# Input loads of 128 rows, an identity and a mask made on GpSimd, and a shorter load queue at the start of a recurrence-plus-experts kernel

## The chip, the cores and the metric

The kernel runs on one core of one Trainium2 chip. The metric is device microseconds for one execution. Before the change it takes 365.24 us (median of 3 runs, 364.93 to 365.54).

## What is computed

A gated linear recurrence (attention without softmax) and then a mixture of experts with one expert for each token. Cut to what matters, with batch 4, 8 heads, 768 steps, head width 48, and 8 experts of 384 x 1024 x 384:

```python
for t in range(S):
    cur = u * k[t] outer v[t]
    y[t] = r[t] @ (state + cur)
    state = w[t][:, None] * state + k[t] outer v[t]
x = y.transpose(0, 2, 1, 3).reshape(B * S, H * D)          # 3072 x 384
logits = x @ w_gate + modality_bias[modality_id]
e = argmax(logits);  g = softmax(logits)[e]
out = g * (relu(x @ w1[e]) @ w2[e])
```

All arithmetic is float32. The mask of the recurrence inside a block of 128 steps is a strict upper triangle, and every transpose on TensorE multiplies by an identity matrix.

## The kernel before, in words

The recurrence is cut into 24 **units** of 128 steps (6 for each batch entry). A unit has all 8 heads: heads lie in pairs, the two heads of a pair in partitions 0 to 47 and 64 to 111, four pairs side by side. One tensor `rkw` holds for each unit 128 rows of 1541 numbers: 512 of r, 512 of k, 517 of w. Rows 48 to 63 and 112 to 127 are padding; the host fills them with zeros for r and k and with ones for w.

`att_iter(i)` works on three units at once. For the unit two ahead, VectorE (DVE) runs two scans over w (`B`, L266, the decay to the end of the block, and `E`, L269, the decay from its start) and a reciprocal (L268); ScalarE (ACT) copies r into PSUM (`pK_r`, L218), DVE multiplies it into `R` (L221), GpSimd (POOL) makes `K` (L224) and `G` (L277). For the unit one ahead, TensorE (PE) transposes K (`pK`, L291), multiplies K by R into the 128x128 blocks `pS` (L305), DVE multiplies these by the mask into `A` (L306), and PE updates the state `st` (L317), which ACT scales and copies (L230, L233). For the unit itself PE forms the output `pY` (L331 from the state, L341 from A), POOL forms `dV` (L273) and DVE adds both into `xp` (`x_rows`, L367). `x_cols` (L374) and `logits` (L380) follow for the unit two behind. Each engine takes its instructions in program order.

Inputs go through four tiles `in0` to `in3` in turn. SyncE (SP) issues all of the loads in program order into one hardware queue; a DMA is spread over 16 DMA engines. `load(n)` (L88) takes 128 rows for the first four units, so that the padding rows are set once, and `64 + D` = 112 rows for the other twenty. The load of unit i+5 is issued behind `att_iter(i)`, when the tile's last reader is done. The load of v (128 rows of 384) goes ahead of it, and from unit 6 on a piece of the first expert's weights (`raw`) goes behind it.

The tile `cs` holds constants: the identity in columns 0 to 127, the mask in columns 128 to 255, and small tables behind these. Before the first unit the program issues the loads of w, r and k of units 0 and 1 with the identity and the mask among them (L101 to L106), PE runs 12 warm-up matmuls on a zeroed tile (L115), and POOL runs ten memsets (L709), the first thing that it does in the kernel's body.

Behind the 24 units the experts follow: blocks of 256 gathered rows, two matmul stages with weights and inputs split into two float32r parts (L621 and L638).

Of the kernel before, what the change touches and what calls it, by code (L numbers as in the profile page):

```python
# [14 lines left out]
ALU = mybir.AluOpType  # L15
AX = mybir.AxisListType

B, H, S, D = 4, 8, 768, 48
P = 128
# [34 lines left out]
def kernel(ctx: ExitStack, tc: tile.TileContext, rkw, vt, wf, cst, mid, wg, bias, w1, w2, out):  # L54
    nc = tc.nc
# [20 lines left out]
    NIN = 4  # L76
    ins = [pa.tile([P, 1541], F32, name=f"in{i}", bufs=1) for i in range(NIN)]
# [8 lines left out]
        return T[tag, n]  # L86

    def load(n, cuts=((0, 1541),)):  # L88
        t, rows = ins[n % NIN], P if n < NIN else 64 + D
        for c0, c1 in cuts:  # L90
            nc.sync.dma_start(out=t[0:rows, c0:c1], in_=rkw[n, 0:rows, c0:c1])

    def loadv(n):
        nc.sync.dma_start(out=wt(n, "v", [P, DM], 4), in_=vt[n * P:(n + 1) * P, :])
# [3 lines left out]
    wm = cp.tile([P, 512], BF16, name="wm")  # L98
    nc.vector.memset(wm, 0.0)
    cs = cp.tile([P, NCST], F32, name="cs")  # L100
    load(0, ((1024, 1541),))  # L101
    nc.sync.dma_start(out=cs[:, 0:P], in_=cst[:, 0:P])
    load(0, ((0, 1024),))
    load(1, ((1024, 1541),))
    nc.sync.dma_start(out=cs[:, P:2 * P], in_=cst[:, P:2 * P])
    load(1, ((0, 1024),))  # L106
    act = cp.tile([1, 1], F32, name="act")
    nc.vector.memset(act, 0.0)
    nc.scalar.activation(out=act, in_=act, func=AF.Exp)
# [22 lines left out]
    for i in range(3):  # L132
        t = wk.tile([P, 4, 2, D], F32, name=f"SPb{i}", bufs=1)
# [811 lines left out]
def _layout(inp):  # L945
    import numpy as np

    r, k, v, w = (np.asarray(inp[n]) for n in "rkvw")

    def tr(a):  # L950
        return a.reshape(B, 4, 2, NCH, P, D).transpose(0, 3, 2, 5, 1, 4)

    W = np.zeros((B, NCH, 2, D, 517), np.float32)
    W[..., :516].reshape(B, NCH, 2, D, 4, 129)[..., 1:] = tr(w)
    rkw = np.zeros((NU, 2, 64, 1541), np.float32)
    rkw[:, :, D:, 1024:] = 1.0
    rkw[:, :, 0:D] = np.concatenate([tr(r).reshape(B, NCH, 2, D, 512), tr(k).reshape(B, NCH, 2, D, 512), W], -1).reshape(NU, 2, D, 1541)
    uu = np.zeros((P, 4, 32), np.float32)
    u = np.asarray(inp["u"]).reshape(4, 2, D)
    for hh in range(2):  # L960
        uu[64 * hh:64 * hh + D, :, hh] = u[:, hh].T
    vt = np.ascontiguousarray(v.transpose(0, 2, 1, 3)).reshape(NT, DM)
    wg = np.asarray(inp["moe_w_gate"])
    c = np.zeros((P, NCST), np.float32)
    c[:, 320:320 + P] = uu.reshape(P, P)
    c[:, 320 + P:] = wg.reshape(KC, P, E).transpose(1, 0, 2).reshape(P, KC * E)
    c[:, 0:P] = np.eye(P)
    c[:, P:2 * P] = np.triu(np.ones((P, P)), 1)
    c[:, 256:264] = np.arange(E) - E
    c[:, 264:288] = np.arange(NU)[None, :] * P + np.arange(P)[:, None]  # L970
    c[:, 288:308] = np.arange(20)
    c[:, 308:316] = np.arange(E) * RS
    mid = np.ascontiguousarray(inp["moe_modality_id"]).astype(np.int64)
    return {
        "rkw": rkw.reshape(NU, P, 1541),
        "vt": vt,
        "wf": np.ascontiguousarray(w).reshape(P, NG * GW),
        "cst": c,
        "mid": mid.view(np.int32).reshape(NU, 2 * P),
        "wg": np.ascontiguousarray(wg),  # L980
        "bias": np.ascontiguousarray(inp["moe_modality_bias"]),
        "w1": np.ascontiguousarray(np.asarray(inp["moe_w1"]).reshape(E, KC, P, FC, P).transpose(0, 2, 3, 1, 4)).reshape(E, P, FC * DM),
        "w2": np.ascontiguousarray(np.asarray(inp["moe_w2"]).reshape(E, FC, P, DM).transpose(0, 2, 1, 3)).reshape(E, P, FC * DM),
    }
# [13 lines left out]
```

## Time and profile before

| what | value |
|---|---|
| median of the runs | 365.24 us |
| the profiled execution | 368.07 us |
| its span, first to last instruction of the program | 366.3 us |
| time of the profiled execution outside the span | 1.77 us |
| mean granted TensorE clock | 0.984 |
| PE busy / DVE busy / ACT busy / POOL busy | 348.2 / 229.3 / 223.8 / 247.1 us |
| share of PE in the chain that ended last | 75% |
| share of DVE in it | 11% |

The durations come from one profiled execution. "Idle before" is the time in which an engine did nothing ahead of an instruction, with what ended that time behind an arrow; "issue" means that the engine waited for nothing that the profile shows. The row "PEclk" has the clock that TensorE was granted, in tenths of full speed; "DMA" the mean busy share of the 16 DMA engines, in tenths, in 40 slices of 9.16 us; an answer by windows has the same as a share of one (a little over 1 where packets overlap at a window's edge). KB in lists of DMA issues are 1024 bytes; GB/s are 10^9 bytes a second. The recurrence fills the span up to about 136 us, the experts the rest.

### The profile page before, as it was taken

The numbers are of one execution on the slowest core, as the hardware profiler recorded it, in microseconds if no ns is written. First come the engines' busy times: TensorE is split into PE (matmuls) and PEld (weight loads), VectorE is DVE, ScalarE is ACT, GpSimd is POOL, SyncE is SP. The second block draws the span as 40 slices with busy tenths as digits, with TensorE's granted clock in tenths as the row PEclk, the third lists the DMA queues.
The fourth block names the chain that finished last, engine by engine and source line by source line (L and its number), as shares of the span: only waits on it lengthen the run. The fifth ranks groups of instructions, "written<-read, shape, count | busy, mean of one in ns | idle before, by whom it ended". The sixth has DMA issues, their size and how long they took to land.

```text
span 366.3 us, 10841 instructions
## 1 busy us (share of the span) xinstructions
PE 348.2 (95%) x4246; PEld 332.0 (91%) x4246; DVE 229.3 (63%) x365; ACT 223.8 (61%) x466; POOL 247.1 (67%) x221
## 2 busy tenths in 40 slices
PE   7889999999889999999999999999999999999993
PEld 2778989898778989999999999999999999999992
DVE  5969999999999836753587471708071716571110
ACT  3647468586364626664676767676867686844340
POOL 4665869998889935875878875564747474728271
PEclk9889999999998999999999999999999999999999
DMA  7994898886786370012255523131312564064200
GB/s 239 316 234 143 239 239 235 235 228 177 227 244 202 129 219 1 2 43 66 86 176 209 181 88 108 46 108 45 108 53 100 162 248 147 28 200 152 105 26 26
DMA packets 20256, 53.28 MB, mean 145 GB/s; under 512 B 2693, under 2 KB 12709, under 8 KB 20196
## 3 DMA queue, kind: packets, MB, share of 16 engines
q1 hardware_dynamic: 17076, 43.04, 40.2%
q0 software_dynamic: 3120, 9.47, 7.0%
q8 instruction: 35, 0.57, 0.6%
q14 instruction: 25, 0.20, 0.2%
HBM read 75.66 MB, written 11.54 MB: 238 GB/s over the span
## 4 chain that ended last, share of the span: by engine, by line
PE 75%; DVE 11%; issue 7%; POOL 3%; DMA 1%; ACT 1%; SPq 0%; POOLq 0%; DVEq 0%; ACTq 0%
PE pS_u L621 20%; PE pY_d L638 13%; PE pX_d L638 13%; PE pT_u L621 9%; PE pS L305 5%; DVE B L266 3%; PE pY L341 3%; DVE A L306 3%; DVE R L221 2%; PE pY L331 2%; PE pK L291 2%; PE pK_x L605 2%; PE pU_st L317 2%; DMA in<-rkw 1%; PE pT L374 1%
## 5 line engine op out<-in xcount | busy, mean ns | idle before, releaser
L207 POOL TENSOR_TENSOR wl<-raw,wh 128x768 fp32r<-128x768 f32 x52 | 96.6, 1868 | 69.5 <-ACT wh L206 69.4
L206 ACT CAST wh<-raw 128x768 fp32r<-128x768 f32 x96 | 79.2, 830 | 35.1 <-PE pX_d L638 24.3
L621 PE MATMUL pS_u<-xh,wh 128*128 128x256 f32 (+1 forms) x198 | 56.3, 284 | 0.0
L621 PE MATMUL pS_u<-xo,wh 128*128 128x256 f32 (+1 forms) x198 | 55.8, 282 | 0.0
L621 PE MATMUL pS_u<-xh,wl 128*128 128x256 f32 (+1 forms) x198 | 55.5, 280 | 0.0
L626 DVE SCALAR_TENSOR_TENSOR hl<-pS_u,hh 128x512 fp32r<-128x512 f32 (+1 forms) x33 | 22.4, 680 | 50.5 <-ACT hh L625 50.5
L207 DVE TENSOR_TENSOR wl<-raw,wh 128x768 fp32r<-128x768 f32 x44 | 49.8, 1132 | 2.8 <-ACT wh L206 1.9
L647 POOL DMA_INDIRECT out<-ot,xl x25 | 32.1, 1282 | 11.0 <-ACT ot L646 5.3
L621 PEld LDWEIGHTS pS_u<-xh,wl 128*128 128x128 f32 x198 | 37.6, 190 | 0.0
L621 PEld LDWEIGHTS pS_u<-xo,wh 128*128 128x128 f32 x198 | 37.2, 188 | 0.0
L621 PEld LDWEIGHTS pS_u<-xh,wh 128*128 128x128 f32 x198 | 37.2, 188 | 0.0
L625 ACT ACTIVATE hh<-pS_u 128x512 fp32r<-128x512 f32 (+1 forms) x33 | 19.5, 591 | 27.5 <-PE pS_u L621 23.7
L626 DVE SCALAR_TENSOR_TENSOR hl<-pT_u,hh 128x512 fp32r<-128x512 f32 (+1 forms) x15 | 10.1, 670 | 39.0 <-ACT hh L625 39.0
L273 POOL TENSOR_TENSOR dV<-v,dT 128x384 f32<-128x384 f32 x24 | 20.0, 834 | 19.7 <-ACT dT L250 8.2
L638 PE MATMUL pY_d<-wh,hh 128*128 128x384 f32 x96 | 33.3, 347 | 0.0
L306 DVE TENSOR_TENSOR A<-pS,cs 128x1024 f32<-128x1024 f32 x24 | 29.2, 1218 | 5.5 <-PE pS L305 5.4
L638 PE MATMUL pX_d<-wh,hh 128*128 128x384 f32 (+1 forms) x96 | 32.3, 336 | 0.0
L638 PE MATMUL pX_d<-wh,hl 128*128 128x384 f32 (+1 forms) x96 | 32.3, 336 | 0.0
L638 PE MATMUL pY_d<-wl,hh 128*128 128x384 f32 x96 | 32.3, 336 | 0.0
L638 PE MATMUL pX_d<-wl,hh 128*128 128x384 f32 (+1 forms) x96 | 32.3, 336 | 0.0
L638 PE MATMUL pY_d<-wh,hl 128*128 128x384 f32 x96 | 32.2, 336 | 0.0
L224 POOL TENSOR_TENSOR K<-in,B 128x512 f32<-128x512 f32 x24 | 28.4, 1185 | 4.2 <-DMA in<-rkw 4.1
(191 smaller groups left out, 894.2 us busy)
## 6 DMA issues: line engine op xcount, KB each, us to landing
raw<-w SPq DMA_DIRECT2D x52, 768.0 KB
in<-rkw SPq DMA_DIRECT2D x20, 674.2 KB
xl<-xs SPq DMA_DIRECT2D x12, 386.0 KB
v<-vt SPq DMA_DIRECT2D x24, 192.0 KB
wg<-wf SPq DMA_DIRECT2D x8, 576.0 KB
raw<-w SPq DMA_DIRECT2D x16, 192.0 KB
xs<-zt SPq DMA_DIRECT2D x8, 193.0 KB
in<-rkw SPq DMA_DIRECT2D x3, 512.0 KB
```

Of the source, the lines that this page charges most:

```text
L206: nc.scalar.copy(out=wh[k][:, sl], in_=raw[k][:, sl])
L207: (nc.vector, nc.gpsimd)[k].tensor_tensor(out=wl[k][:, sl], in0=raw[k][:, sl], in1=wh[k][:, sl].bitcast(F32), op=ALU.subtract)
L224: nc.gpsimd.tensor_tensor(out=wt(a, "K", [P, 4, P]), in0=quarters(k), in1=quarters(T["B", a][:, 1:517])[:, :, 1:129], op=ALU.mult)
L266: nc.vector.tensor_tensor_scan(out=Bt[:, 516:0:-1], data0=w[:, 516:0:-1], data1=d1[:, 516:0:-1], initial=0.0, op0=ALU.mult, op1=ALU.max)
L273: nc.gpsimd.tensor_tensor(out=dV, in0=T["v", z].rearrange("p (a b) -> p a b", a=H), in1=T["dT", z].rearrange("p a b -> p (a b)")[:, :, Non ...
L305: nc.tensor.matmul(out=pS[:, hh, p], lhsT=K[q, p], rhs=R[q, p], start=True, stop=True)
L306: nc.vector.tensor_tensor(out=A.rearrange("p a b c -> p (a b) c"), in0=pS.rearrange("p a b c -> p (a b) c"), in1=mask[:, None, :].to_broad ...
L621: nc.tensor.matmul(out=pp[:, i], lhsT=wsrc[0][:, f, c * P:(c + 1) * P], rhs=xsrc[:, c], start=(n == 0), stop=(n == 3 * KC - 1))
L625: nc.scalar.activation(out=hh, in_=pp, func=AF.Relu)
L626: nc.vector.scalar_tensor_tensor(out=hl, in0=pp, scalar=0.0, in1=hh.bitcast(F32), op0=ALU.max, op1=ALU.subtract)
L638: nc.tensor.matmul(out=X["y", q][j][0:h.shape[-1]], lhsT=h, rhs=wsrc[1][:, f], start=(f == 0 and n == 0), stop=(f == FC - 1 and n == 2))
L647: ins = nc.gpsimd.indirect_dma_start(out=out[:, :], out_offset=bass.IndirectOffsetOnAxis(ap=xl[0:n, j, DM + 1:DM + 2].bitcast(I32), axis=0 ...
```

## The change

Three edits. `load` takes all 128 rows for every unit, where units 4 to 23 took 112. The two loads of the identity and the mask are gone, so the loads of r and k of units 0 and 1 stand right behind their w. POOL makes identity and mask: a memset of 128x256 to one, and two `affine_select` of 128x128, which keep the diagonal and the part above it and write zero elsewhere. The host no longer fills these columns.

```diff
     def load(n, cuts=((0, 1541),)):
-        t, rows = ins[n % NIN], P if n < NIN else 64 + D
         for c0, c1 in cuts:
-            nc.sync.dma_start(out=t[0:rows, c0:c1], in_=rkw[n, 0:rows, c0:c1])
+            nc.sync.dma_start(out=ins[n % NIN][:, c0:c1], in_=rkw[n, :, c0:c1])
...
-    load(0, ((1024, 1541),))
-    nc.sync.dma_start(out=cs[:, 0:P], in_=cst[:, 0:P])
-    load(0, ((0, 1024),))
-    load(1, ((1024, 1541),))
-    nc.sync.dma_start(out=cs[:, P:2 * P], in_=cst[:, P:2 * P])
-    load(1, ((0, 1024),))
+    load(0, ((1024, 1541), (0, 1024)))
+    load(1, ((1024, 1541), (0, 1024)))
+    nc.gpsimd.memset(cs[:, 0:2 * P], 1.0)
+    for c0, op in ((0, ALU.is_equal), (P, ALU.is_gt)):
+        v = cs[:, c0:c0 + P]
+        nc.gpsimd.affine_select(out=v, in_=v, compare_op=op, fill=0.0, base=0, pattern=[[1, P]], channel_multiplier=-1)
```

The order of the instructions on SP at the start of the kernel before, from its first load; `in0_88` and `in1_89` are the input tiles of units 0 and 1, where 128x517 is w and 128x1024 is r and k:

```order
L91 DMA in0_88<-rkw 128x517
L102 DMA cs_94<-cst 128x128
L91 DMA in0_88<-rkw 128x1024
L91 DMA in1_89<-rkw 128x517
L105 DMA cs_94<-cst 128x128
L91 DMA in1_89<-rkw 128x1024
L94 DMA v0_152<-vt 128x384
```

The same place in the changed kernel (line numbers are lower by one from here on):

```order
L90 DMA in0_88<-rkw 128x517
L90 DMA in0_88<-rkw 128x1024
L90 DMA in1_89<-rkw 128x517
L90 DMA in1_89<-rkw 128x1024
L93 DMA v0_153<-vt 128x384
```

The two `cs` loads are gone; r and k of unit 0 move from third to second place, those of unit 1 from sixth to fourth.

SP a little later in the kernel before, where the tiles are loaded for the second time (units 4 and 5, into `in0` and `in1`):

```order
L91 DMA in3_91<-rkw 128x1541
L94 DMA v2_239<-vt 128x384
L91 DMA in0_88<-rkw 112x1541
L94 DMA v3_317<-vt 128x384
L91 DMA in1_89<-rkw 112x1541
```

And in the changed kernel:

```order
L90 DMA in3_91<-rkw 128x1541
L93 DMA v2_240<-vt 128x384
L90 DMA in0_88<-rkw 128x1541
L93 DMA v3_318<-vt 128x384
L90 DMA in1_89<-rkw 128x1541
```

Nothing moves there; the loads from unit 4 on have 128 rows in place of 112.

POOL from the first instruction of the kernel's body, before; `ISA` is an instruction that names the library of GpSimd code that the following operations come from, and K0, G0 are the first unit's:

```order
L709 MEMSET SPb0_124 128x384
L709 MEMSET SPb1_125 128x384
L709 MEMSET SPb2_126 128x384
L709 MEMSET onesb_130 128x128
L709 MEMSET one8_133 128x8
L709 MEMSET ersb_132 128x8
L709 MEMSET zt_134 128x386
L709 MEMSET zt_134 128x1
L709 MEMSET glo_128 128x1
L709 MEMSET ghi_129 128x1
L224 ISA
L224 TENSOR_TENSOR K0_175<-in0_88,B0_170 128x512
```

And in the changed kernel:

```order
L102 MEMSET cs_94 128x256
L105 ISA
L105 AFFINE_SELECT cs_94<-cs_94 128x128 x2
L708 MEMSET SPb0_125 128x384
L708 MEMSET SPb1_126 128x384
L708 MEMSET SPb2_127 128x384
```

A memset, the library instruction and the two selects stand ahead of the ten memsets, which keep their order; K0 follows directly behind the last of these. The order on PE, DVE and ACT is unchanged.

More of the change, by code (lines that the diff above doesn't have):

```diff
@@ L966, in _layout @@
     c[:, 320 + P:] = wg.reshape(KC, P, E).transpose(1, 0, 2).reshape(P, KC * E)
-    c[:, 0:P] = np.eye(P)
-    c[:, P:2 * P] = np.triu(np.ones((P, P)), 1)
     c[:, 256:264] = np.arange(E) - E
```

## The prediction

> **What bounds the kernel now.** The experts, from about 136 us on, are left alone; what the change can move is how late they begin. So I read the recurrence: first who VectorE waits for up to 130 us.
>
> ```profile
> DVE A L306 <- PE pS L305: 5.4, 5, 2.7
> ...
> DVE R L221 <- ACT pK_r L218: 1.0, 1, 1.0
> ```
>
> (Total us, times, longest.) Then its busy time in the stretches between the longest waits: each row has the stretch, its length, the busy us and instructions of PE, PE's weight loads, DVE, ACT and POOL, then PE's granted clock, the DMA share and GB/s.
>
> ```profile
> 7.20:24.47 17.27, 13.43 (x241) 12.16 (x242) 16.99 (x21) 9.21 (x27) 11.46 (x11) 0.87 1.04 291
> 27.16:56.40 29.24, 28.17 (x651) 25.96 (x652) 28.79 (x39) 18.55 (x60) 19.80 (x25) 1.00 0.73 206
> 56.90:126.00 69.10, 64.89 (x1472) 59.60 (x1474) 67.05 (x105) 42.76 (x134) 61.44 (x71) 0.98 0.74 213
> ```
>
> DVE is busy for 98%, 98% and 97% of these. From its first R to the last units it is a chain without slack, so a microsecond by which it starts earlier, or waits less, is a microsecond at the end. Its timeline shows the places where it does wait.
>
> ```profile
> 4.96 1.23 DVE L269 TENSOR_TENSOR_SCAN E<-in,pX_d 128x516 f32<-128x516 f32 x1
> 7.20 0.69 DVE L221 TENSOR_TENSOR R<-pK_r,E 128x512 f32<-128x512 f32 x1 [1.01 <-ACT pK_r L218]
> ...
> 10.42 1.20 DVE L306 TENSOR_TENSOR A<-pS,cs 128x1024 f32<-128x1024 f32 x1
> ...
> 23.94 0.53 DVE L367 TENSOR_TENSOR xp<-pY,dV 128x384 f32<-128x384 f32 x1
> 27.16 1.22 DVE L306 TENSOR_TENSOR A<-pS,cs 128x1024 f32<-128x1024 f32 x1 [2.68 <-PE pS L305]
> ...
> 32.03 1.23 DVE L306 TENSOR_TENSOR A<-pS,cs 128x1024 f32<-128x1024 f32 x1
> ...
> 56.91 1.22 DVE L306 TENSOR_TENSOR A<-pS,cs 128x1024 f32<-128x1024 f32 x1 [0.47 <-PE pS L305]
> ```
>
> Three waits matter: 1.01 us at the start, 2.68 us at 24.5 and 0.47 us at 56.4. The last two are caused by TensorE, whose timeline says why.
>
> ```profile
> 8.55 1.16 PE L305 MATMUL pS<-R,K 64*128 64x128 f32 x16
> ...
> 20.45 0.73 PE L341 MATMUL pY<-v,A 128*64 128x48 f32 x19
> 22.53 0.56 PE L341 MATMUL pY<-v,A 128*64 128x48 f32 x13 [1.35 <-issue]
> ...
> 25.14 1.98 PE L305 MATMUL pS<-R,K 64*128 64x128 f32 x16
> ...
> 28.46 1.09 PE L341 MATMUL pY<-v,A 128*64 128x48 f32 x32
> ...
> 53.19 0.24 PE L331 MATMUL pY<-SPb,R 128*64 128x96 f32 x1 [0.61 <-issue]
> ```
>
> PE stops at 21.2 us between the 19th and the 20th of 32 equal matmuls, for 1.35 us. Their operands were there for the first 19, and the releaser is "issue": no engine's signal. It stops again near 52.6 us for 0.61. What it lacks is then the instructions themselves, which come by DMA too:
>
> ```profile
> q8 instruction: 35, 0.57, 0.6%
> ```
>
> 35 packets with 0.57 MB, 16 KB each, in a queue of their own on the same 16 engines. The stretches around the stops, and the clock:
>
> ```profile
> 0.00:10.50 10.50, 7.81 (x61) 3.89 (x62) 6.70 (x12) 3.65 (x7) 5.84 (x18) 1.00 0.79 261
> 10.50:13.50 3.00, 1.40 (x21) 1.17 (x20) 2.97 (x5) 2.23 (x8) 1.91 (x3) 0.95 1.05 408
> 13.50:28.00 14.50, 13.05 (x233) 11.81 (x233) 11.64 (x15) 7.53 (x23) 8.80 (x8) 0.77 1.04 232
> 24.00:27.00 3.00, 3.00 (x22) 2.59 (x20) 0.48 (x2) 1.56 (x3) 3.00 (x3) 0.52 1.03 238
> 51.00:54.00 3.00, 2.39 (x70) 2.10 (x67) 3.00 (x5) 1.73 (x6) 1.50 (x2) 1.00 0.97 239
> ```
>
> The granted clock is 0.52 in 24 to 27 us, right behind the first stop, and the 16 matmuls of pS take 1.98 us there against 1.16 at 8.55. The DMA share is about 1 in both stretches with a stop: the engines that must bring PE's instructions are full.
>
> **Why they are full.** The GB/s of those rows differ by 408 to 232 at the same full share. I put names to the bytes by the sizes of the issues.
>
> ```profile
> in<-rkw SPq DMA_DIRECT2D x20, 674.2 KB
> v<-vt SPq DMA_DIRECT2D x24, 192.0 KB
> ...
> raw<-w SPq DMA_DIRECT2D x16, 192.0 KB
> ...
> in<-rkw SPq DMA_DIRECT2D x3, 512.0 KB
> in<-rkw SPq DMA_DIRECT2D x3, 258.5 KB
> in<-rkw SPq DMA_DIRECT2D x1, 770.5 KB
> ...
> cs<-cst SPq DMA_DIRECT2D x2, 64.0 KB
> cs<-cst SPq DMA_DIRECT2D x1, 108.0 KB
> ```
>
> Units 0 to 3, `cs` and three loads of v are 4 x 770.5 + 236 + 3 x 192 = 3894 KB = 3.99 MB. By 13.5 us 261 x 10.5 + 408 x 3 = 3.96 MB had moved. So the 408 GB/s are loads of 128 rows, and the stretch behind, 232 x 14.5 = 3.36 MB, is units 4 to 7 and three v: 4 x 674.2 + 576 = 3273 KB = 3.35 MB. These are the first loads of 112 rows. The fall by 43% comes exactly where the row count changes.
>
> **The change part by part.**
>
> *Shorter queue at the start.* SP needs some 0.47 us for an issue:
>
> ```profile
> 0.71 0.39 SPq L91 DMA_DIRECT2D in<-rkw  x1
> 1.16 0.42 SPq L102 DMA_DIRECT2D cs<-cst  x1
> 1.63 0.90 SPq L91 DMA_DIRECT2D in<-rkw  x2
> ```
>
> r and k of unit 0 are issued at 1.16 in place of 1.63, and 64 KB go from ahead of them. In the chain that ended last they are the first piece:
>
> ```profile
> 1.63 4.92 DMA in<-rkw
> 6.58 0.60 ACT pK_r L218
> ```
>
> Landing moves from 6.55 to about 6.1, R from 7.20 to 6.73: **0.47 us**. At least 0.2 (64 KB at 261 GB/s take 0.25, if the issue hides), at most 0.98, since E ends at 6.19. B of unit 1 follows at once, and w of unit 1 moves up as well, by the same issue.
>
> *GpSimd.* POOL's first work moves back behind a memset, the library instruction and two selects:
>
> ```profile
> 0.71 1.13 POOL L709 MEMSET SPb<- 128x384 f32 x3 [0.29 <-POOLq L991]
> ...
> 2.54 0.10 POOL L709 MEMSET ghi<- 128x1 f32 x1
> 6.70 1.17 POOL L224 TENSOR_TENSOR K<-in,B 128x512 f32<-128x512 f32 x1 [4.06 <-DMA in<-rkw]
> ```
>
> The ten memsets take 0.71 to 2.64, 1.93 us; a memset of 128x256 takes two thirds of one of the three, 0.25. A select of 128x128 is not in the trace. Bounds: 0.10, the small memset, and 1.17, K over four times the elements; I take 0.30, a quarter of K. The library instruction stood inside the 4.06 us ahead of K: 0 to 4.06, and I take about 0, as the gap ends with the DMA that released ACT at 6.58. K can then start at 0.71 + 0.25 + 0.6 + 1.93 = 3.5, ahead of r and k at 6.1. The cover is the landing of r and k, and its cost is nil. Identity and mask are ready by 1.6, far ahead of pK and A.
>
> *128 rows.* Each later load has 96.3 KB more, but at 408 GB/s it takes 1.93 us where 674.2 KB at 232 took 2.98. Units 4 and 5, two v and small ones (about 1.97 MB) are through by 13.2 + 4.8 = 18 us, and unit 6, issued when its tile is free, about 2 us later; then the queue is empty. PE's instruction packet finds short queues. Without the stop pY ends at 20.45 + 1.09 = 21.54. In the next unit A followed pY's end (28.46 + 1.09 = 29.55) by 2.48 us, so A could start at 24.02, and DVE is free at 24.47: **2.68 us** fall away whole. Next to be late is DVE itself. For the stop at 52.6 us the load of an iteration becomes 770.5 + 192 + 192 (weights) KB = 1.18 MB in 4.87 us, 60% of 408 GB/s; but here weights share the queue. Between 0 and 0.47 I take the middle, **0.24**.
>
> Sum: 0.47 + 2.68 + 0.24 = 3.4 us. The span goes from 366.3 to 362.9, the profiled execution, 1.77 longer, from 368.07 to 364.7; taken off the median, 365.24 - 3.4 = **361.9 us**. The median lies 2.83 below the profiled execution, so a part of the stops may belong to profiling.
>
> **The rivals.**
>
> *Only the start gains.* The stop stays, or happens only under the profiler: 365.24 - 0.47 = 364.8. For it: the queue is full for all of the 14.5 us from 13.5 on, and PE stops once. Against it: both stops lie at a full share, none in the emptier rest.
>
> *Half.* The stop shrinks, but the idle time still takes the clock down: half of 2.68 and the start, 363.4.
>
> *More bytes, no speed.* The rate fell for another reason than the row count, and each load costs 14% more. Then four loads add 4 x 96.3 KB = 0.39 MB, 1.7 us at 232 GB/s, to the queue ahead of PE's instructions; the wait grows by as much, and less the 0.47 the time is 366.5, slower. It decides if the new loads run below 232 x 128 / 112 = 265 GB/s. For it: the clock of PE also fell near 13 us. Against it: in 51 to 54 us the clock is 1.00 and the rate 239. The Trainium skill ("SBUF — State Buffer", Door 1: The DMA port swizzle) speaks for this rival: which of 16 ports a row uses depends on its number, and by that table rows 0 to 111 already reach all 16, with four ports half used. By it 112 rows would run at 7/8 of the rate of 128, 357 of 408 GB/s, and take as long; the 232 GB/s of this trace are far below, so more than the count of ports is at work.
>
> *GpSimd late.* The library instruction costs up to 4.06 and a select up to 1.17: K starts at 0.71 + 0.25 + 4.06 + 2.34 + 1.93 = 9.29. pS ended 9.71 - 7.87 = 1.84 after K, so A would start at 12.30 against 10.42 now. If the stops stay too, 367.1. It decides when library and selects together pass 4.05 us (K after 6.94, A after 9.95). Against it: K's wait ended 0.12 us after ACT's, for the same load. The Trainium skill ("GPSIMD Engine Reference", Instruction dispatch) gives about 6 us for the first call into freshly loaded code; by that K before could not have started until 8.59, and it started at 6.70.
>
> *Nothing moves*, 365.2.
>
> **How the numbers follow.** The sum as forecast 0.51, half 0.14, only the start 0.18, nothing 0.03, more bytes 0.09, GpSimd 0.05. A measurement tells about 0.2%, 0.73 us, from no change: faster 0.51 + 0.14 = 0.65, same 0.18 + 0.03 = 0.21, slower 0.14. The range goes from the largest sum, 0.98 + 2.68 + 0.47 = 4.13 or 361.1, to 365.2, where nothing moves; it leaves out the two slower cases.
>
> **What would show it.** Right: R of unit 0 near 6.7; over 350 GB/s from 13.5 us until the queue is empty near 20; no "issue" row of over a microsecond on PE; DVE's wait for pS at 24.5 gone; A of the fourth unit near 24.0. Wrong: the rate stays near 232, a stop of PE at another place, or K's wait with no DMA behind it.

## The result, and the profile after

The changed kernel takes 364.09 us (median of 19 runs, 363.76 to 366.78), the kernel before 365.83 us (19 runs beside them, 364.93 to 367.98). The ratio is 0.9949, with an interval from 0.9935 to 0.9963: faster by 1.9 us, at least 1.35 and at most 2.4. Forecast were 361.9 us and a gain of 3.3 to 3.4 us. The direction was right, the size was not: a little over half of the gain came.

In the profiled execution, though, all of it came and more: 363.79 us against 368.07, 4.28 us less, with a span of 362.1 against 366.3 and a granted clock of 0.996 against 0.984. (Seven slow executions, at 370.62, 370.68, 370.81, 372.22, 372.69, 432.01 and 669.92 us, are left out of the ratios below.)

DVE's timeline of the changed kernel, with the same instructions as those shown of the kernel before (start, duration, engine, line, operation; a bracket would be a wait):

```profile
4.94 1.23 DVE L268 TENSOR_TENSOR_SCAN E<-in,pX_d 128x516 f32<-128x516 f32 x1
6.27 0.69 DVE L220 TENSOR_TENSOR R<-pK_r,E 128x512 f32<-128x512 f32 x1
9.49 1.20 DVE L305 TENSOR_TENSOR A<-pS,cs 128x1024 f32<-128x1024 f32 x1
...
23.39 1.21 DVE L305 TENSOR_TENSOR A<-pS,cs 128x1024 f32<-128x1024 f32 x1
...
52.49 1.21 DVE L305 TENSOR_TENSOR A<-pS,cs 128x1024 f32<-128x1024 f32 x1
```

All three waits are gone: R follows E directly, and neither the A of the fourth unit nor that of the tenth has a bracket. The first A is 0.93 us earlier than before (10.42), the fourth 3.77 (27.16) and the tenth 4.42 (56.91). So the start brought 0.93 us, the stop near 21 us 2.84, the one near 52 us 0.65.

TensorE's timeline at the place of the first stop, and the changed kernel's stretches in the columns of the prediction's table (us, busy time of PE, weight loads, DVE, ACT and POOL, then PE's granted clock, DMA share, GB/s):

```profile
19.44 1.09 PE L340 MATMUL pY<-v,A 128*64 128x48 f32 x32
...
21.80 1.16 PE L304 MATMUL pS<-R,K 64*128 64x128 f32 x16
```

```profile
10.50:13.50 3.00, 2.06 (x38) 1.80 (x39) 2.93 (x5) 2.20 (x6) 1.89 (x3) 1.00 1.04 424
13.50:20.00 6.50, 4.99 (x128) 4.52 (x124) 6.43 (x9) 4.79 (x15) 4.71 (x5) 1.00 0.97 370
20.00:28.00 8.00, 8.00 (x183) 7.39 (x180) 7.86 (x11) 4.98 (x14) 5.03 (x5) 1.00 0.56 165
51.00:54.00 3.00, 3.00 (x82) 2.88 (x82) 3.00 (x4) 2.45 (x8) 3.00 (x4) 1.00 0.86 262
```

The 32 matmuls of pY stand in one piece, and pS takes 1.16 us where it took 1.98. From 13.5 to 20 us the loads run at 370 GB/s, where the kernel before had 232, and from 20 us on the share is 0.56: the queue no longer stays full. The clock is 1.00 in every one of these stretches.

GpSimd's start, and SyncE's first issues:

```profile
0.78 0.31 POOL L102 MEMSET cs<- 128x256 f32 x1 [0.29 <-POOLq L988]
1.17 0.54 POOL L105 TENSOR_SCALAR_AFFINE_SELECT cs<-cs 128x128 f32<-128x128 f32 x2
...
3.49 0.10 POOL L708 MEMSET ghi<- 128x1 f32 x1
5.01 1.18 POOL L223 TENSOR_TENSOR K<-in,B 128x512 f32<-128x512 f32 x1 [1.42 <-DVE in L267]
```

```profile
0.78 1.82 SPq L90 DMA_DIRECT2D in<-rkw  x4
```

A select takes 0.27 us, and the library instruction at most the 0.08 us between the memset's end at 1.09 and the first select. The ten memsets end at 3.59, and K, free at 5.01, now waits for VectorE and no longer for a load.

What DVE waits for on PE up to 130 us, as grouped by the view of waits (us in total, times, longest):

```profile
DVE A L305 <- PE pU_st L316: 1.7, 2, 1.0
...
DVE A L305 <- PE pS L304: 0.9, 1, 0.9
```

Before it was 5.4 us in five waits for pS. The two for pU_st, 0.99 us at 111.3 and 0.72 at 116.9, are new in this execution; TensorE has an "issue" stop of 0.42 us ahead of each, and they are what lies between the 4.42 us gained at the tenth unit and the 3.22 that are left at the unit behind the second of them (120.15 against 116.93). Such stops from about 99 us on go with the comparison and not with the kernel: the profiles of the experiments e5 to e11 and e15 to e17 below all show them, for both kernels, and those of e1 to e4 and e12 to e14 show none.

So each step of the forecast can be seen in the profile, and yet the median gained less than half of what the profiled execution did. The question is what a typical execution of the kernel before holds.

### The profile page after: what moved, and what is told of

Same layout as the page of the kernel before. It is cut to its first block, busy times and chain, and to the rows that moved or that the text cites. A ratio compares the mean times of both kernels' runs of the same rounds, so it can differ in the third digit from the quotient of the medians.

```text
span 362.1 us, 10843 instructions
## 1 busy us (share of the span) xinstructions
PE 345.2 (95%) x4246; PEld 328.9 (91%) x4246; DVE 229.7 (63%) x365; ACT 223.4 (62%) x466; POOL 248.5 (69%) x224
## 4 chain that ended last, share of the span: by engine, by line
PE 75%; DVE 10%; issue 7%; POOL 3%; ACT 2%; DMA 1%; POOLq 0%; DVEq 0%; ACTq 0%; SPq 0%
PE pS_u L620 20%; PE pY_d L637 14%; PE pX_d L637 14%; PE pT_u L620 9%; PE pS L304 4%; DVE B L265 3%; DVE A L305 3%; PE pY L340 3%; PE pY L330 3%; DVE R L220 2%; PE pK L290 2%; PE pK_x L604 2%; PE pR_x L379 1%; PE pU_st L316 1%; PE pT L373 1%
## 5 line engine op out<-in xcount | busy, mean ns | idle before, releaser
L206 DVE TENSOR_TENSOR wl<-raw,wh 128x768 fp32r<-128x768 f32 x44 | 51.6, 1172 | 2.9 <-ACT wh L205 1.9
L229 ACT ACTIVATE pU_st<-pU_st,B 128x48 f32<-128x48 f32 x80 | 22.0, 275 | 17.4 <-PE pU_st L316 11.5
```

The costliest lines, as they stand in the source:

```text
L206: (nc.vector, nc.gpsimd)[k].tensor_tensor(out=wl[k][:, sl], in0=raw[k][:, sl], in1=wh[k][:, sl].bitcast(F32), op=ALU.subtract)
L229: nc.scalar.activation(out=st[:, p], in_=st[:, p], func=AF.Copy, scale=tot[:, p, 0:1])
```

## The experiments

Two theories at the start. The first: the change works as forecast (rows and start each contribute), and the profiled execution of the kernel before held longer stops than its typical ones. The rival: only the earlier start counts, or only the row count, and the rest of the profiled gain was chance. Each ratio below stands against the kernel before, run on the same chip in the same comparison.

**The parts alone.** 128 rows with the old start; the new start with 112 rows; the kernel before as a control.

```
e1_rows: the kernel before, but
-        t, rows = ins[n % NIN], P if n < NIN else 64 + D
-            nc.sync.dma_start(out=t[0:rows, c0:c1], in_=rkw[n, 0:rows, c0:c1])
+            nc.sync.dma_start(out=ins[n % NIN][:, c0:c1], in_=rkw[n, :, c0:c1])

e2_start: changed kernel, but
+        t, rows = ins[n % NIN], P if n < NIN else 64 + D
-            nc.sync.dma_start(out=ins[n % NIN][:, c0:c1], in_=rkw[n, :, c0:c1])
+            nc.sync.dma_start(out=t[0:rows, c0:c1], in_=rkw[n, 0:rows, c0:c1])

e3_before: the kernel before, once more
```

> Only the 128 rows; the queue at the start and the constants as before. Theory A (the stop of TensorE at 21 us is there in all executions, but its length differs, and the profiled execution before had a long one): no issue row over 1 us on PE up to 60 us, over 350 GB/s from 13.5 us until the queue is empty, R of unit 0 still near 7.2, and the median 0.6 to 1.5 us below before. Theory B (the stop belongs to the profiled execution alone, the gain of the median comes from the start): the rate rises all the same, the median moves by less than 0.3 us.

> Only the start (shorter load queue, identity and mask on GpSimd); units 4 to 23 loaded with 112 rows. Both theories: R of unit 0 at 6.3, which is 0.95 us earlier, and 232 GB/s behind 13 us. A: the median is 0.8 to 1.0 us below before and the stop of PE near 20 us stays, in some executions longer than in others. B: the median falls by all of 1.7 us.

> The kernel before once more, nothing changed, for a second profiled execution and a spread of times. A: executions differ by up to 3 us with the granted clock (0.98 to 0.995), and in this profile the wait of DVE near 24.5 us is not 2.68 us but anything from 0 to 3. B: each profiled execution has the 2.7 us and lies near 368, while the timed ones lie near 365.5 with no spread by clock.

Measured: the rows alone 365.17 us, ratio 0.9964 (0.9942 to 0.9987); the start alone 364.80, ratio 0.9952 (0.9926 to 0.9978); the kernel before 365.86, ratio 0.9984 (0.9958 to 1.001). So each part gains by itself, about 1.3 and 1.8 us, and the two together (1.9) bring less than their sum. The rows came as theory A had them (with 329 GB/s where over 350 was expected, at a share of 0.89), the start as theory B had it (1.7), and the control's profiled execution took 368.24 us among others of 364.87 to 368.04. The profile of the rows alone:

```profile
13.50:20.00 6.50, 6.33 (x119) 5.68 (x117) 6.36 (x9) 4.05 (x13) 4.57 (x6) 0.77 0.89 329
20.00:28.00 8.00, 8.00 (x190) 7.51 (x188) 7.86 (x11) 5.44 (x18) 5.03 (x5) 1.00 0.67 226
```

```profile
20.49 1.09 PE L340 MATMUL pY<-v,A 128*64 128x48 f32 x32
```

The clock is 0.77 from 13.5 to 20 us, as it was before, and there is no stop: the low clock was not the cause of the stop, nor of the low rate.

What the stop waits for can be read from the instruction packets (queue q8) in the traces. In the kernel before the first of them lands at 21.12 us, and TensorE goes on at 22.53. In all nine executions with a stop near 21 us (the kernel before, e2, e3, e4, e6, e12, e15, e16 and e17) TensorE goes on 1.30 to 1.58 us after this packet has landed. In e1 TensorE is as far as in the kernel before (this pY starts at 20.49 and 20.45 us), but the packet lands at 18.46, and no stop follows. So it is the late packet that makes the stop.

The start alone keeps the slow loads (242 GB/s from 13.5 to 20 us) and keeps a stop, a shorter one; TensorE's and DVE's timelines:

```profile
21.51 0.56 PE L341 MATMUL pY<-v,A 128*64 128x48 f32 x13 [0.53 <-issue]
```

```profile
24.55 1.22 DVE L306 TENSOR_TENSOR A<-pS,cs 128x1024 f32<-128x1024 f32 x1 [0.27 <-PE pS L305]
```

**What is slow about 112 rows.** The changed kernel, with the loads from unit 4 on as two of 64 rows each, in the same number of bytes.

```
e4_halves: changed kernel, but in load()
+            for q in ((0, P),) if n < NIN else ((0, 64), (64, P)):
+                nc.sync.dma_start(out=t[q[0]:q[1], c0:c1], in_=rkw[n, q[0]:q[1], c0:c1])
```

> The changed kernel, but the loads from unit 4 on are two DMAs of 64 rows each (0 to 63 and 64 to 127): the bytes of the changed kernel in another split over the engines. Theory P (what slows 112 rows is that several DMA engines write to the same part of SBUF at the same time, and halves do that too): 200 to 260 GB/s from 13.5 us, a stop of PE near 20 us, time as with the start alone. Theory Q (it is the seven rows for each engine, and four or eight are well): over 350 GB/s, no stop, time as the changed kernel, within 0.4 us.

Measured: 376.14 us, ratio 1.026 (1.0216 to 1.0304), slower by 9.5 us. Its stretches, and its stop on TensorE:

```profile
13.50:20.00 6.50, 4.99 (x130) 4.52 (x126) 6.43 (x9) 4.72 (x15) 4.92 (x5) 1.00 1.02 211
...
24.00:27.00 3.00, 3.00 (x21) 2.65 (x21) 0.05 (x1) 1.72 (x4) 2.55 (x3) 0.50 1.05 224
```

```profile
22.50 0.88 PE L342 MATMUL pY<-v,A 128*64 128x48 f32 x13 [2.13 <-issue]
```

Same bytes, same engines, all of them full: 211 GB/s in place of 370, and the stop is back (2.13 us; DVE then waits 3.85); later ones take 1.74 and 3.07 us. The rate and the stop came as theory P had them, the time didn't, and its reason is not shown. The packets are of one size, a row of 6164 bytes, but between 14 and 19 us each of them takes 440 ns on average in the kernel before and 465 in e4, against 255 in the changed kernel. So the rate hangs on the rows that a load covers, whether on their number or on which they are, and the longer stop came with the lower rate. The Trainium skill ("SBUF — State Buffer", Door 1: The DMA port swizzle) says that rows 0 to 63 reach only 8 of the 16 ports, and measures 196 GB/s for them; the 211 GB/s here are near that. For 112 rows the ports of the same table give an estimate of 7/8 of the full rate, and the 232 GB/s contradict it; why 112 rows are so slow is open.

**Full queue or slow packets?** Three more loads of 768 KB, with 128 rows and never read, behind the loads of units 4 to 6, so that the engines stay full; and 128 rows only for the first eight units.

```
e7_full_queue: changed kernel, and in its loop over the units
+        if -1 <= i < 2:
+            nc.sync.dma_start(out=raw[0][:, 4 * (i % 2):4 * (i % 2) + 4, :]..., in_=w1[0, :, 0:4 * DM])

e8_early: changed kernel, but
+        t, rows = ins[n % NIN], P if n < 2 * NIN else 64 + D
```

> The changed kernel with three more loads of 768 KB (128 rows, into a tile of the weights that is loaded again before it is read) behind the input loads of units 4, 5 and 6, so that the load queue stays full beyond 21 us with rows that are fast. Theory Q (a full queue is enough to hold up TensorE's instructions): an issue row of PE of 0.5 us or more between 18 and 25 us, and 0.5 to 2.5 us slower than the changed kernel. Theory M (it needs the slow packets of the 112-row loads): over 350 GB/s up to 24 us at a share near 1, no such row, and the time of the changed kernel within 0.4 us.

> The changed kernel, but only units 4 to 7 have the 128 rows; units 8 to 23 go back to 112. Theory E (the rows bring their gain in the full stretch from 13 to 28 us alone): the time of the changed kernel within 0.3 us, no stop near 21 us. Rival L (the later loads matter as much, by the stop near 52 us): 0.4 to 0.8 us slower than the changed kernel, with an issue row of 0.3 us or more on PE between 40 and 60 us.

Measured: 364.67 us, ratio 0.9963 (0.994 to 0.9986), and 364.38 us, ratio 0.9957 (0.9938 to 0.9976). The full queue's stretch:

```profile
13.50:28.00 14.50, 13.70 (x304) 12.51 (x302) 13.62 (x18) 9.15 (x29) 8.83 (x10) 0.95 1.01 397
```

The engines are nearly as full as before the change (1.01, then 1.04, for the same 14.5 us), with no "issue" row before 100 us. So the prediction's word "full" was not the whole condition: a full queue of loads of 128 rows stops nothing, one of 112 rows does. The median of e7 lies 0.58 us above the changed kernel's, a little more than the 0.4 that theory M allowed; no stop explains that. With 128 rows for eight units only, the stop at 21 us is gone and one near 50 us stays:

```profile
49.94 0.24 PE L331 MATMUL pY<-SPb,R 128*64 128x96 f32 x1 [1.05 <-issue]
```

DVE waits 0.91 us behind it, and still the median is within 0.3 us of the changed kernel's, so the loads of units 4 to 7 make up most of what the rows bring.

**Is a profiled execution of the kernel before always long?** Three more of the kernel before, unchanged.

> The kernel before, unchanged, once more: the execution whose profile is kept beside several that are only timed. Theory F (the execution with the full profile is disturbed, and its stops are longer): the profiled one lies near 368, with waits of DVE for pS of 2.4 to 2.7 us at 24.5 us, the others near 365.5 to 366. Theory S (chance: about one execution in five of this kernel lies over 368): the profiled one lies among the others, most likely at 365 to 367, with a wait of 0 to 2 us.

> The same as the run ahead of it, for a fourth profiled execution of the kernel before. F: near 368 again. S: anywhere from 365 to 369, and not 368 both times.

> The kernel before, one profiled execution more beside the two with 15 warm-ups. By the theory of the idle gap 368 to 370 us with a stop of more than a microsecond; if the chip or the hour decides, like its two neighbours.

Measured: e5 366.48 us in the median (ratio 1.0003, 0.9968 to 1.0038) with 370.19 in its profiled execution; e6 370.45 in its profiled execution, too few others for a median; e17 366.11. Four of the five were long, and the fifth is a usual one, so a profile need not make an execution long; whether it makes a long one likelier is not shown. Side by side (the warm-up matmuls' duration; TensorE's idle time behind them, up to pK; pK's duration; then DVE's waits and the "issue" stops ahead of them; us):

| execution | time | warm-ups | idle | pK | wait of first A | stop at 21, wait | stop at 50 to 53, wait |
|---|---|---|---|---|---|---|---|
| the one shown | 368.07 | 5.30 | 1.52 | 0.63 | none | 1.35, 2.68 | 0.61, 0.47 |
| e3 | 368.24 | 5.30 | 1.36 | 0.63 | none | 1.24, 2.37 | 1.15, 1.01 |
| e5 | 370.19 | 4.20 | 2.48 | 1.09 | 0.63 | none | 1.42, 3.86 |
| e6 | 370.45 | 4.40 | 2.27 | 1.02 | 0.56 | 0.60, 0.34 | 1.44, 3.86 |
| e17 | 366.11 | 4.15 | 2.15 | 1.09 | 0.63 | 0.88, 0.62 | none (0.53 at 45, no wait) |

The stop changes its place and its length from one execution to the next. Its price has two steps. At 21 us a stop costs DVE its length less 0.26 us (0.53 to 0.27, 0.60 to 0.34, 0.88 to 0.62); the slack of 0.26 us is A's. Where the clock falls behind it, the price leaps: 1.35 us cost 2.68, 1.59 more than 1.35 - 0.26. Here are TensorE's and DVE's timelines and the stretch behind the stop of e17, where the clock stays at 1.00 (it was 0.52 in those 3 us in the execution that the prediction used):

```profile
22.20 0.56 PE L341 MATMUL pY<-v,A 128*64 128x48 f32 x13 [0.88 <-issue]
```

```profile
25.25 1.22 DVE L306 TENSOR_TENSOR A<-pS,cs 128x1024 f32<-128x1024 f32 x1 [0.62 <-PE pS L305]
```

```profile
24.00:27.00 3.00, 3.00 (x77) 2.84 (x78) 2.38 (x5) 2.41 (x8) 2.69 (x3) 1.00 0.92 284
```

Of the 148 executions of the kernel before that stand beside the experiments and the result, 22 take 368.0 us or more. The one that the prediction was worked out from is of that seventh. Four of five profiled executions in it would come by chance about twice in a thousand (an estimate from 22 of 148), so profiling may have a part; e17 shows that it doesn't always. The theory of the idle gap, which follows below, had 368 to 370 us for e17, too, and missed.

**The start: who makes the identity, and how late may it be?** Identity and mask loaded in one piece behind r and k of unit 1, as the changed kernel orders them; and 16 selects in place of two, to try the prediction's bound (K may start up to 6.94 us).

```
e9_order: changed kernel, but
+    nc.sync.dma_start(out=cs[:, 0:2 * P], in_=cst[:, 0:2 * P])
-    (memset and affine_select)

e10_selects: changed kernel, but
-    for c0, op in ((0, ALU.is_equal), (P, ALU.is_gt)):
+    for c0, op in 8 * ((0, ALU.is_equal), (P, ALU.is_gt)):

e11_after: the changed kernel, once more
```

> The changed kernel, but identity and mask come by one load of 128 KB behind r and k of unit 1, and GpSimd does not make them. Theory O (the gain of the start is the order of the queue alone): R of unit 0 near 6.3, time of the changed kernel within 0.3 us. Rival G (it needs GpSimd: the identity lands too late for the first transposes, or 128 KB more push back the loads behind): pK of unit 0 waits for the load beyond 7.1, and 0.3 to 1 us slower than the changed kernel.

> The changed kernel with 14 more selects on GpSimd ahead of its memsets (each repeats one of the two, 0.27 us or a little more). By the slack worked out before (K of unit 0 may start up to 1.93 us later than its 5.01 until A is late): GpSimd is free at 7.4 to 8.5 instead of 3.6, K starts then, A of unit 0 comes 0.5 to 1.6 us later than 9.49, with DVE waiting for pS, and the time rises by as much. Rival: K has more slack, and neither A nor the time moves.

> The changed kernel once more, nothing else, beside the two others. If the first, fully profiled execution is disturbed only where the load queue is full of 112-row loads, the profiled time lies within 1 us of the median, as it did before (363.79 and 364.09), with no issue row over 1 us on PE. Rival: it is disturbed here too, and lies 2 us or more above the median.

Measured: e9 366.01 us, ratio 0.9979 (0.9953 to 1.0006); e10 365.85, ratio 0.9975 (0.9941 to 1.001); e11 364.16, ratio 0.9938 (0.9913 to 0.9963). TensorE's timeline of e9, and GpSimd's and DVE's of e10:

```profile
8.28 0.63 PE L287 MATMUL pK<-cs,K 128*128 128x128 f32 x4 [1.81 <-DMA cs<-cst]
```

```profile
1.17 4.00 POOL L105 TENSOR_SCALAR_AFFINE_SELECT cs<-cs 128x128 f32<-128x128 f32 x16
...
7.02 1.19 POOL L223 TENSOR_TENSOR K<-in,B 128x512 f32<-128x512 f32 x1
```

```profile
10.12 1.22 DVE L305 TENSOR_TENSOR A<-pS,cs 128x1024 f32<-128x1024 f32 x1 [0.46 <-PE pS L304]
```

The prediction's bound of 6.94 went with an A at 9.95. A comes at 9.49 in the changed kernel, which puts the bound at 6.48 (9.49 less the 1.17 of K and the 1.84 that the prediction has between K and the end of pS). K at 7.02 is 0.54 us past that and makes the first A wait 0.46 us, so the sum holds. The loaded identity makes TensorE wait till 8.28. Both lose about 0.6 us in the profiled execution (364.37 and 364.40 against 363.78) and 1.7 to 1.9 in the median. Something at the start costs typical executions more than their profiles show.

**The idle time behind the warm-up matmuls.** The table above has a candidate. The same 12 warm-up matmuls take 5.30 us in some executions and 4.15 to 4.40 in others, and TensorE then idles till pK. With up to 1.85 us of idle time pK takes 0.63 to 0.68 us; with 2.15 and more it takes 1.02 to 1.09 at a granted clock near 0.5, and the first A is 0.56 to 0.63 us late. The length of the gap alone doesn't decide, though. In e2 and e7 it is the second pK that is slow, behind 1.58 us, and the second A waits 0.68; in the kernel before the second pK took 0.63 behind 1.60. TensorE in e2:

```profile
11.46 1.09 PE L291 MATMUL pK<-cs,K 128*128 128x128 f32 x4 [1.58 <-DVE R L221]
```

In the changed kernel the first pK is at 7.1 to 7.3 us, so the idle time stays at 1.85 or less even behind short warm-ups (e11). If the idle time is a cause, more warm-up matmuls must help where pK is late.

```
NWARM = 12  ->  e12_before_warm  15 (the kernel before)
                e13_order_warm   16 (e9)
                e14_after_warm   13 (the changed kernel)
                e18_rows_warm    15 (e1)
e15_warm_again, e16_warm_third: e12 again, one profiled execution each
```

> The kernel before with 15 warm-up matmuls in place of 12, which fills the 1.52 us of idle TensorE ahead of the first transposes. Theory C (idle time at the start lowers the clock in typical executions, and that is what they lose over the least time): the median comes down to 365.0 to 365.5, 0.7 to 1.4 us below the kernel before, and the least time stays near 364.9. Rival D (the loss comes from the instruction stops under the full queue of 112-row loads): median as before, within 0.4 us.

> The kernel of e9 (changed kernel, constants loaded behind r and k of unit 1) with 16 warm-up matmuls, which fills its 1.8 us of idle TensorE. C: the median falls from 366.0 to 364.4 to 364.9, near its profiled 364.4. D: no 112-row loads are in it, so D has nothing to explain its loss; if neither holds, the median stays at 365.7 to 366.2.

> The changed kernel with 13 warm-up matmuls, which fills most of its 0.58 us. C: at most 0.2 us faster than the changed kernel, as its executions lie near the least time already. D: no change. It would be the fastest kernel of all if it comes below 364.1.

> The kernel before with 15 warm-up matmuls once more, one profiled execution. If the idle 1.52 us of TensorE ahead of its first transposes make the stops of the kernel before long (in four profiled executions without the three matmuls: 368.07 to 370.45 us), this execution lies below 366 as the first one did (364.68), with no issue row over 0.7 us on PE. If that one was only a lucky execution, it lies at 368 to 370 with a stop over a microsecond.

> As the run ahead of it: below 366 us and no issue row over 0.7 us by the theory of the idle gap, 368 to 370 by luck.

> The kernel of 128 rows with the old start and 15 warm-ups in place of 12. By the theory of the idle gap the median falls from its 365.17 us (ratio 0.9964) by about 0.7, as the kernel before did with the same three matmuls: 364.3 to 364.7, ratio near 0.994. If the gap matters only together with slow loads, the median stays near 365.2 and the ratio near 0.9965.

Measured, each beside the kernel without the added matmuls:

| kernel | 12 warm-ups: us (lowest, highest), ratio | more: us (lowest, highest), ratio |
|---|---|---|
| before, 15 | 366.02 (364.57, 369.31), 1 | 365.33 (364.31, 367.30), 0.9968 (0.9937 to 0.9999) |
| e9, 16 | 366.01 (364.37, 367.00), 0.9979 (0.9953 to 1.0006) | 364.07 (363.50, 364.64), 0.9932 (0.9906 to 0.9958) |
| changed, 13 | 364.16 (363.69, 365.87), 0.9938 (0.9913 to 0.9963) | 363.61 (363.37, 364.75), 0.9927 (0.99 to 0.9953) |
| e1, 15 | 365.17 (364.18, 366.81), 0.9964 (0.9942 to 0.9987) | 364.86 (364.46, 365.16), 0.9943 (0.992 to 0.9967) |

All four medians fall, most for e9, where pK is latest; but its two intervals overlap by a hair (0.9953, 0.9958), and those of the other rows overlap widely. The highest times fall in all four rows, too (of 29 and 12 executions in the first row, of 12 and about as many in the others). For e1 the median falls by 0.3 us and the ratio by 0.0021, which is 0.8 us, near the 0.7 expected; the profiled execution of its kernel with 15 warm-ups took 432.01 us and tells nothing here. The mean granted clock of an execution is higher with more warm-ups in every row: 0.988 and 0.991, 0.9885 and 0.995, 0.9935 and 0.9945, 0.988 and 0.994 in the median. So the clock is a likely way for the gain, but no profile shows it: in e13's the first A still waits 0.78 us, as the identity lands late. In profiles of the kernel before with 15 warm-ups the idle time is 0.49 to 1.07 us, pK takes 0.63 and the first A waits in none of them. The three took 364.68, 365.62 and 367.02 us; the last one missed what was expected of it, with a stop of 1.59 us near 51 us and a wait of 1.38. So in these three the first A is in time, and the stops are still there. One of the three, e12, at the place of the first stop (TensorE, DVE):

```profile
20.91 0.61 PE L341 MATMUL pY<-v,A 128*64 128x48 f32 x15 [0.31 <-issue]
```

```profile
24.06 1.23 DVE L306 TENSOR_TENSOR A<-pS,cs 128x1024 f32<-128x1024 f32 x1
```

A stop of 0.31 us hides nearly whole in the slack; DVE shows no wait. The stop that cost 2.68 us in the prediction's profile costs nothing here.

The lowest median of all is the changed kernel with 13 warm-ups, 363.61 us; it beats the kernel before (at most 0.9953), and whether it beats the changed kernel the intervals don't tell.

## Why the prediction was right and wrong

*The start, 0.47 us.* Too small: 0.93. The bound of 0.98 was right: r and k landed at 4.87 us (6.1 was forecast), before E ended, R waits for nothing, and DVE's own chain became the limit. On top comes what the forecast did not have at all: with pK nearly a microsecond earlier, TensorE's idle time stays under 2 us, and the 0.6 us by which the first A was late in three of five executions of the kernel before go as well (in e2 and e7, with the same start, the second A was 0.68 late instead).

*GpSimd, nothing.* Right. A select costs 0.27 us (0.30 taken), the memset 0.31 (0.25 taken), the library instruction next to nothing, and K is at 5.01. The prediction's bound of 6.94 is 6.48 for an A at 9.49, so K is 1.5 us inside it; K at 7.02 costs 0.46.

*128 rows.* Right in mechanism: 370 GB/s after 232, a queue that is no longer full from 20 us on, an instruction packet that lands at 17.5 us in place of 21.1, no stop, and the fourth A at 23.39 (near 24.0 was forecast, with half the gain of the start). "More bytes, no speed" fell with the first load: e4 shows that the same bytes in loads of 64 rows are slow. The condition "full" was too wide; e7's full queue stops nothing.

*2.68 us for the stop at 21 us: here it failed.* The prediction worked this wait out of one profiled execution of 368.07 us and then took the sum off the median of 365.24. It saw the 2.83 us between the two and gave them one sentence ("a part of the stops may belong to profiling"), but no term. An execution that takes 365.24 us can't hold the waits of one that takes 368.07, unless something else in it is 2.8 us shorter. The stop is no constant of the kernel: 1.35, 1.24, 0.88, 0.60 us or none, for waits of 2.68, 2.37, 0.62, 0.34 and 0; 1.59 of the 2.68 were the low clock behind it, which e6 and e17 are spared. By e17, the profiled execution that lies nearest to the medians, the first A would move from 10.62 to 9.49, 1.13 us, and 0.62 would go with the stop: an estimate of 1.75 us. Measured are 1.35 to 2.4. That a typical execution has the stop of e17 is not shown, as no execution without a profile shows its stops. Whether profiling itself lengthens them, as the prediction supposed for a part, stays open.

*0.24 us for the stop at 52 us.* The middle of two ends, gone whole in the profiled execution; in the kernel before it runs from none to 3.86 us of waiting, so no single number stands for it.

*The rivals.* "Half" (a gain of 1.8 us) came closest in size, but not for its reason, a clock that still falls: it is 1.00 in all of the changed kernel's stretches above. Its other executions need not be so: 11 of the 19 had a mean granted clock under 0.994, down to 0.983. Whether its size came by luck can't be told. "Only the start gains" is refuted by e1, which gains 1.3 us with the old start; yet the start alone, e2, gained 1.8, more than any case of the prediction gave it. The two together bring 1.9 in place of 3.1. In e2's one profile the stop is short (0.53), so the early start may take from the stops as well; how the 1.9 us divide between the two can't be told within these intervals.

Open stay three things: why each packet of a load of 112 rows takes so long; why four of five profiled executions of the kernel before belong to its slowest seventh; and why e9 and e10 lose 1.7 to 1.9 us in the median, of which their profiles show 0.6. Their two profiled executions are of the kind with long warm-ups (5.30 us); what the short ones cost there was not seen. For e9 the loss goes with the clock: its two executions at a mean granted clock of 0.994 took 364.37 and 364.64 us, its ten others, at 0.982 to 0.993, 365.44 to 367.00.

## What to carry to other kernels

Ahead of taking a sum off the median, compare the profiled execution's time with the median: where they differ by as much as the gain, the waits of that profile aren't those of a typical execution, and a second profile is worth more than a finer sum. Try loads of all 128 rows, even if some are padding: here 14% more bytes went at 1.6 times the rate. And look at a wait in two parts, the stop and the slow clock behind it, and at the slack that swallows short stops.

## What the runs showed of the hardware

- With the DMA engines busy all the time, loads of 112 rows ran at 232 to 266 GB/s (13.5 to 20 us), of 128 rows at 362 to 425, of twice 64 rows at 210 to 224. A packet of 6164 bytes took 440, 255 and 465 ns on average (14 to 19 us; the kernel before, the changed kernel, e4).
- TensorE's instructions arrived late behind slow loads (stops of 0.2 to 3.1 us; the first one ended 1.30 to 1.58 us after an instruction packet had landed), and up to 100 us not behind loads of 128 rows that kept the same engines as full (397 GB/s, share 1.01). From 99 us on, stops of 0.2 to 0.5 us stand in the profiles of some comparisons, for both kernels, and in none of others; their cause is open.
- Idle for up to 1.85 us ahead of the first pK, TensorE went on at full clock; idle for 2.15 us, it took 1.7 times as long (1.09 against 0.63 us; the granted clock was 0.50 from 7.9 to 8.9 us in e17). Behind the second gap 1.58 us went with 1.09 us in e2 and 1.60 with 0.63 in the kernel before. TensorE and DVE in e5, with 2.48 us:

```profile
7.85 1.09 PE L291 MATMUL pK<-cs,K 128*128 128x128 f32 x4 [2.48 <-POOL K L224]
```

```profile
11.00 1.22 DVE L306 TENSOR_TENSOR A<-pS,cs 128x1024 f32<-128x1024 f32 x1 [0.63 <-PE pS L305]
```

  The Trainium skill ("TensorE: Matmul & The Clock Gate", What's actually happening) has the clock fall after at least one idle window of about 3.4 us; here 2.15 us were enough, and 1.58 in e2. It also says that the window runs free of the kernel's start, which fits the other observation: the same 12 warm-up matmuls took 4.12 to 5.30 us from one execution to another.
- The library instruction of GpSimd ahead of the first select cost at most 0.08 us, a select of 128x128 f32 0.27 and 0.25 each in a row of 16.
